# Sinkhorn-sorted attention and a bilinear feed-forward: pieces of unused matmuls, an early part of an output tile, and a token-on-partition mix for the last six pairs

## The chip, the cores and the metric

The kernel runs on one core of a Trainium2 chip. The metric is device time in microseconds (us) of one execution; lower is better. TensorE is called PE here (its weight loads PEld), VectorE DVE, ScalarE ACT, GpSimd POOL, and SyncE SP.

## The reference

Four batches, eight heads, 768 tokens, 64 elements a head. The tokens of a head stand in eight blocks of 96. Cut to what is computed:

```
P = sort_net                                  # 4 x 8 x 8 x 8
repeat 5 times:
    P = exp(P - rowmax);  P = P / rowsum;  P = P / columnsum
k_sorted = P mixes the 8 blocks of k;  v_sorted = P mixes the 8 blocks of v
scores = (q_block @ k_sorted_block^T) / 8     # inside each block of 96
attn   = softmax(scores)
x      = attn @ v_sorted_block                # 3072 tokens x 512
a = x @ w_a;  b = x @ w_b                     # 512 -> 1536
out = (a * b) @ w_out                         # 1536 -> 512, float32
```

## The kernel before, in words

Heads are worked on in pairs: pair g (0 to 15) has heads 2g and 2g + 1, and four pairs make a batch. Pair 0 to 3 is batch 0, and so on. All matmuls are bf16 with float32 sums.

The **Sinkhorn chain** (five rounds on ACT and DVE) comes first. Meanwhile PE does unused matmuls on a zero tile `warm` (`keep_busy`, L168) and turns q of the first pairs (`turn_q`). Each round after the first has one small matmul on `rsum`, so that the unused ones behind it start in step with the chain. The final P is spread by `to_columns` (L448) and `spread` into `s_all`, for each head a 128 x 128 matrix.

The **mix** multiplies it with k or v. A token's place in its 128-row chunk is on the partitions when it is loaded. `stage_mix` (L281) takes a 64-column chunk of k or v of one head as weights and `s_all` as the moving operand, 12 matmuls of 128 columns for k and 12 for v. The result has head elements on the partitions. ACT copies it into `kT`, DVE and ACT copy it into `vT`, in block order. v needs tokens on the partitions later: `turn_v` does this on PE for pair 4, a DMA transpose on the SP queue for pairs 5 and up, into `vs`. `stage_scores` (L302) then makes the scores and ACT the exponential `eT`; `stage_o` (L231, with `one_o`) multiplies with `vs` and DVE divides; `to_xT` sends the result through a DMA transpose into `xT`. Batch 0 is done in two halves of four blocks (`half_mix` to `half_x`), with PE transposes in place of the DMA's.

The **feed-forward** of batch b needs its `xT`. `ffn_ab` makes one step: eight matmuls of 384 columns (`ab_mms`, L332), four for a and four for b; ACT casts a (L352) and DVE multiplies into `hT` (L353). An output tile (`ffn_out`, L377) is two steps of six matmuls of 512 columns, then a copy to `o_sb` and a store. A batch has 24 such steps of the first kind and 12 of the second.

The **order** on PE, POOL, SP, ACT and DVE is written out by hand. While batch b's feed-forward runs, the attention of batch b + 1 is put between its steps: `units_full` lists units, c (mix), s (scores), o (output) of a pair, and `paced` spreads them over the steps. In the first batch some matmuls of the first feed-forward tiles are begun ahead (`begun`), three of their four parts each, and end later.

Loads with a cast from float32 go on POOL's queue. From pair 6 on, the mix of pair g is followed by a one-element POOL copy `gate` that waits for `kT`, and then by the load of pair g + 2, so that loads are not issued too early. q of pairs 6 and up is put in order by POOL (`pair_q`, L246) and turned by a DMA transpose (`stage_q`, L252). Buffers that matter: `kT`, `vT`, `eT`, `vs` have three each (pair number modulo 3), pool `psA` two PSUM tiles, `psF` four, `hT` two, `o_sb` three.

Of the kernel before, what the change touches and what calls it, by code (L numbers as in the profile page):

```python
# [9 lines left out]
FP32 = mybir.dt.float32  # L10
# [12 lines left out]
def kernel(  # L23
# [250 lines left out]
    def stage_mix(g, what, engines):  # L274
        src2 = loaded[g][0 if what == "k" else 1]
        to = (kTs if what == "k" else vTs)[g % NBUF]
        pitch, whole = (BLK, S + PAD) if what == "k" else (P, NB * P)
        mix = psA.tile([P, 2, 512], FP32, tag="A", name="mix")
        for c in range(NCH):
            for e in range(2):  # L280
                nc.tensor.matmul(  # L281
                    mix[e * D:(e + 1) * D, c // 3, c % 3 * P:(c % 3 + 1) * P],
                    lhsT=src2[:, e, c * D:(c + 1) * D],
                    rhs=s_all[:, 2 * g + e], start=True, stop=True)
        for hf, eng in enumerate(engines):
            n = 2 // len(engines)
            for u in range(n):
                d1 = _ap(to, (hf + u) * 3 * CG, [[whole, P], [CG, 3], [pitch, NB], [1, CG]])
                s1 = _ap(mix, (hf + u) * 512, [[1024, P], [P, 3], [CG, NB], [1, CG]])
                copy(eng, d1, s1)  # L290
        if what == "v" and g > HP:
            nc.sync.dma_start_transpose(out=vss[g % NBUF][:, :, V0:V0 + P],
                                        in_=to.rearrange("p i t -> p (i t)"))

    def stage_scores(g):
        kT, qT, eT = kTs[g % NBUF], st[g, "qT"], eTs[g % NBUF]
# [37 lines left out]

    def hT_of(b):
        if b not in hTs:
            hTs[b] = ffp.tile([P, KO, S], BF16, tag="hT", name="hT")
        return hTs[b]

    def ffn_ab(b, m, t, begun=()):  # L340
# [15 lines left out]
    def ffn_last(b, c):  # L356
        hT = hTs[b]
        rows = out[b * S:(b + 1) * S, :].rearrange("(p c) n -> c p n", c=NCH)
        for n0, n1, eng, queue in ((0, 384, "act", nc.sync), (384, DMODEL, "dve", nc.scalar)):
            po = psF.tile([P, 512], FP32, tag="F", name="po")  # L360
            for m in range(KO):
                nc.tensor.matmul(po[:, 0:n1 - n0], lhsT=hT[:, m, c * P:(c + 1) * P],  # L362
                                 rhs=w_out_sb[:, m, n0:n1], start=(m == 0), stop=(m == KO - 1))
            o_sb = ffp.tile([P, 512], FP32, tag="o_sb", name="o_sb", bufs=3)
            copy(eng, o_sb[:, 0:n1 - n0], po[:, 0:n1 - n0])
            queue.dma_start(out=rows[c][:, n0:n1], in_=o_sb[:, 0:n1 - n0])

# [14 lines left out]
        return [lambda: part(0), lambda: part(1)]  # L382

    def store(b, c, po):
        o_sb = ffp.tile([P, DMODEL], FP32, tag="o_sb", name="o_sb", bufs=3)
        copy("act" if c % 2 == 0 else "dve", o_sb, po)
        if b == 0:
            h, u = divmod(c, 3)
            for c2 in range(2):
                nc.sync.dma_start(  # L390
                    out=_ap(out, (h * PH * NCH + 2 * u + c2) * DMODEL,
                            [[NCH * DMODEL, PH], [1, DMODEL]]),
                    in_=o_sb[c2 * PH:(c2 + 1) * PH])
        else:
            rows = out[b * S:(b + 1) * S, :].rearrange("(p c) n -> c p n", c=NCH)
            nc.sync.dma_start(out=rows[c], in_=o_sb)


    with tc.manual_schedule(engines={ET.PE, ET.Pool, ET.SP}):
        with tc.manual_schedule(engines={ET.Activation, ET.DVE}):  # L400
# [3 lines left out]
            p_rep = const.tile([BH, NB * NB, CG // 2], FP32, name="p_rep")  # L404
            pc_ps = psA.tile([P, NB, BH], FP32, tag="A", name="pc_ps")
            heat = psA.tile([P, 2, 512], FP32, tag="A", name="heat")
            keep_busy(heat[:, 0], 8)
            for it in range(5):
                nc.scalar.activation(out=p_nat, in_=p_nat, func=AF.Exp)
                if it == 2:  # L410
                    turn_q(0, "act")
                if it == 3:
                    turn_q(1, "act")
                if it == 4:
                    turn_q(2, "act")
                    turn_q(3, "act")
                if it == 2:
                    with nc.allow_low_precision("sum of one one and zeros"):
                        nc.vector.reduce_sum(
                            out=mask, in_=_ap(ident, 0, [[P, P], [1, CG], [CG, NB]]),  # L420
                            axis=AX.X)
                nc.vector.reduce_sum(out=rsum, in_=p_nat, axis=AX.X)
                nc.vector.reciprocal(out=rsum, in_=rsum)
                if it > 0:
                    nc.tensor.matmul(heat[0:NB, 1, 0:NB], lhsT=rsum, rhs=rsum,
                                     start=True, stop=True)
                    keep_busy(heat[:, 0], (0, 4, 3, 2, 4)[it])
# [55 lines left out]
            half_o(0, 2)  # L483
            half_scores(0, 3)
            half_v(0, 3)
            half_x(0, 2, "act")
            half_o(0, 3)
            begun = [psF.tile([P, 512], FP32, tag="F", name="pf") for _ in range(3)]
            begun += [psA.tile([P, 2, 512], FP32, tag="A", name="two")[:, 0] for _ in range(2)]
            for n, (m, w_sb) in enumerate(((0, w_a_sb), (0, w_b_sb), (1, w_a_sb),  # L490
                                           (1, w_b_sb), (2, w_a_sb))):
                if n == 3:
                    half_x(0, 3, "act")
                ab_mms(begun[n], w_sb, 0, m, 0, range(KA - 1))


        for c in range(4, 6):
# [30 lines left out]
            us.append(lambda: half_x(1, HP - 1, "dve"))  # L528
            return us

        def units_full(b):
            g0, us = b * HP, []

            def c_(g):
                if g < 2 * HP - 2:
                    turn_q(g)
                stage_mix(g, "k", ("act",))
                stage_mix(g, "v", ("dve", "act"))
                if 2 * HP - 2 <= g < B * HP - 2:
                    nc.gpsimd.tensor_copy(out=gate, in_=kTs[g % NBUF][0:1, 0:1])  # L540
                    load_pair((g + 2) // HP, (g + 2) % HP)

            def s_(g):
                stage_scores(g)
                if g == HP:
                    turn_v(g)
                if g in (HP, HP + 1):
                    stage_q(g + 2)
                if 2 * HP <= g + 1 < B * HP:
                    pair_q(g + 1)  # L550
                    stage_q(g + 1)

            def o_(g):
                stage_o(g)
                to_xT(g)

            for u, n in ((c_, 0), (s_, 0), (c_, 1), (s_, 1), (c_, 2), (o_, 0), (s_, 2), (c_, 3),
                         (o_, 1), (s_, 3), (o_, 2), (o_, 3)):
                us.append(lambda u=u, g=g0 + n: u(g))
            return us  # L560

        def interleave(steps, units, spare, slow=0):
            n, done = len(steps), 0
# [4 lines left out]
                    units[done]()  # L568
                    done += 1

        def paced(ab, po, units, spare):
            steps = ab + po
            total = len(steps) - 2 * spare
            done = 0
            for now, step in enumerate(steps, 1):
                step()
                while done < len(units) and done * total < now * len(units):
                    units[done]()
                    done += 1

        steps = [lambda: ffn_ab(0, 0, 0, begun[0:2]), lambda: ffn_ab(0, 1, 0, begun[2:4]),
                 lambda: ffn_ab(0, 2, 0, begun[4:5])]
# [3 lines left out]
        for b in range(B):  # L586
            ab = [lambda m=m, t=t, b=b: ffn_ab(b, m, t)
                  for m in range(KO) for t in range(2) if b > 0 or t == 1]
            po = [f for c in range(NCH) for f in ffn_out(b, c)]
            paced(ab, po, units_full(b + 1) if b + 1 < B else [], 3 if b == 0 else 2)  # L590


# [28 lines left out]
```

The softmax here doesn't subtract the row's maximum and nothing guards it: scores larger than these inputs give would overflow.

## Time and profile before

| | |
|---|---|
| median of 12 runs | 245.81 us (245.53 to 246.31) |
| the profiled execution | 246.07 us |
| its span, first to last instruction | 244.3 us |
| PE busy | 237.0 us, 2234 matmuls |
| ACT, DVE, POOL busy | 104.5, 109.2, 61.5 us |
| granted TensorE clock | 1.0 |
| DMA transposes | 33 on SP's queue |
| last feed-forward of a batch ends near | 85, 139.6, 194 us for batches 0, 1, 2 |

Times inside the kernel count from the start of the span. In a view of the chain, a row has the start, the length, and the engine, tile and line; in a table of stretches the columns after the length are the busy times of PE, PEld, DVE, ACT and POOL, with the number of instructions in brackets, then the granted clock, the DMA engines' mean share and GB/s. A matmul's own duration is a latency: matmuls overlap in the array, so what one costs in a row of its like is the distance of the starts.

### The profile page before, as it was taken

Reading aid. Unit: us, or ns where it says so; the run is one execution under the profiler, and the core shown is the slowest. Engines: PE = TensorE matmul, PEld = TensorE weight load, DVE = VectorE, ACT = ScalarE, POOL = GpSimd, SP = SyncE. Lnnn points to the kernel's source line nnn. Section 1 sums busy time; section 2 is a strip of 40 time slices with the busy share of each in tenths; the row PEclk is TensorE's granted clock in tenths of the full one; section 3 lists DMA queues with packets and bytes.
Section 4 is the critical chain, followed back from the end, with each engine's and each line's share of the span. In section 5 each row is a group of like instructions: output and inputs, shape, how many; then the busy total and the mean of one; then the engine's idle time right before and its main releaser. Section 6 shows DMA issues by size and latency. Waiting matters only on the chain.

```text
span 244.3 us, 5487 instructions
## 1 busy us (share of the span) xinstructions
PE 237.0 (97%) x2234; PEld 137.0 (56%) x2246; DVE 109.2 (45%) x258; ACT 104.5 (43%) x204; POOL 61.5 (25%) x88
## 2 busy tenths in 40 slices
PE   7899999999999999999999999999999999999994
PEld 2466666666545466666654466666654465655442
DVE  6675466554436144454524234454525144344110
ACT  3664764466730065646430175636330133333001
POOL 8875579613230043240400053110000000000000
PEclk9999999999999999999999999999999999999999
DMA  5999999998999659994883457926224310000132
GB/s 80 201 198 197 197 200 201 202 119 84 168 152 195 137 97 126 157 150 70 120 131 118 119 101 123 157 54 67 43 79 122 114 46 0 0 3 1 43 129 86
DMA packets 53929, 28.02 MB, mean 115 GB/s; under 512 B 30736, under 2 KB 50960, under 8 KB 53904
## 3 DMA queue, kind: packets, MB, share of 16 engines
q0 software_dynamic: 20944, 14.16, 41.1%
q1 hardware_dynamic: 32816, 13.45, 28.9%
q8 instruction: 17, 0.28, 0.5%
q14 instruction: 8, 0.07, 0.1%
q10 hardware_dynamic: 144, 0.07, 0.1%
HBM read 28.32 MB, written 6.29 MB: 142 GB/s over the span
## 4 chain that ended last, share of the span: by engine, by line
PE 94%; DVE 3%; issue 1%; ACT 1%
PE pf L332 51%; PE po L377 24%; PE mix L281 4%; PE o_ps L231 3%; PE sc L302 2%; PE heat L168 2%; PE mixh L180 2%; PE po L362 1%; PE vs_ps L208 1%; PE sc L195 1%; PE xt_ps L222 1%; PE two L332 1%; PE q_ps L260 1%; DVE xp L237 1%; DVE o_sb L164 0%
## 5 line engine op out<-in xcount | busy, mean ns | idle before, releaser
L353 DVE TENSOR_TENSOR hT<-a_sb,pf 128x384 bf16<-128x384 bf16 x95 | 52.6, 554 | 73.8 <-PE pf L332 46.4
L332 PE MATMUL pf<-xT,w_a_sb 128*128 128x384 bf16 x380 | 77.9, 326 | 0.0
L332 PE MATMUL pf<-xT,w_b_sb 128*128 128x384 bf16 x380 | 77.4, 326 | 0.0
L352 ACT CAST a_sb<-pf 128x384 bf16<-128x384 f32 x95 | 45.5, 479 | 60.9 <-PE pf L332 41.3
L377 PE MATMUL po<-w_out_sb,hT 128*128 128x512 bf16 x265 | 61.3, 379 | 0.6
L332 PEld LDWEIGHTS <-w_b_sb 128*128 128x128 bf16 x384 | 37.5, 98 | 24.6
L332 PEld LDWEIGHTS <-w_a_sb 128*128 128x128 bf16 x384 | 34.9, 98 | 22.3
L377 PEld LDWEIGHTS <-hT 128*128 128x128 bf16 x276 | 26.2, 98 | 30.1
L162 ACT COPY o_sb<-po 128x512 f32<-128x512 f32 (+1 forms) x13 | 7.5, 578 | 46.8 <-PE po L377 45.2
L164 DVE COPY o_sb<-po 128x512 f32<-128x512 f32 (+1 forms) x12 | 7.9, 656 | 35.1 <-PE po L377 26.2
L307 ACT ACTIVATE eT<-sc 96x768 bf16<-96x768 f32 x24 | 18.1, 802 | 6.8 <-PE sc L302 6.8
L540 POOL COPY gate<-kT 1x1 bf16<-1x1 bf16 x8 | 1.4, 181 | 76.1 <-ACT kT L162 76.1
L237 DVE TENSOR_TENSOR xp<-o_ps,rec 96x512 bf16<-96x512 f32 x24 | 15.9, 684 | 0.6 <-DVE rec L235 0.2
L162 ACT CAST kT<-mix 128x384 bf16<-128x384 f32 x24 | 10.3, 482 | 7.9 <-PE mix L281 7.9
L95 POOL DMA_DIRECT2D k<-in_k_dram x16 | 11.6, 722 | 5.5 <-PE pf L332 2.3
L231 PEld LDWEIGHTS <-eT 96*128 96x128 bf16 x256 | 10.3, 97 | 3.1 <-DVE xp L237 0.6
L95 POOL DMA_DIRECT2D v<-in_v_dram x16 | 11.5, 718 | 2.1 <-PE pf L332 0.8
L235 DVE RECIPROCAL rec<-o_ps 96x8 f32<-96x8 f32 x32 | 5.6, 189 | 13.8 <-PE o_ps L231 13.8
L231 PE MATMUL o_ps<-vs,eT 96*128 96x65 bf16 x256 | 11.3, 193 | 0.1
L246 POOL COPY qc<-q 128x768 bf16<-128x768 bf16 x10 | 8.3, 834 | 8.1 <-DMA q<-in_q_dram 8.1
L168 PE MATMUL heat<-warm 128*128 128x512 bf16 x20 | 7.7, 530 | 1.4 <-DVE warm L77 1.3
L95 POOL DMA_DIRECT2D q<-in_q_dram x12 | 8.6, 713 | 1.5 <-DMA w_a_sb<-in_moe_w_a_dram 0.6
(80 smaller groups left out, 154.0 us busy)
## 6 DMA issues: line engine op xcount, KB each, us to landing
out_dram<-o_sb SPq DMA_DIRECT2D x17, 256.0 KB, 2.0
k<-in_k_dram POOLq DMA_DIRECT2D x16, 192.0 KB, 5.4
v<-in_v_dram POOLq DMA_DIRECT2D x16, 192.0 KB, 6.7
q<-in_q_dram POOLq DMA_DIRECT2D x12, 192.0 KB, 6.9
w_a_sb<-in_moe_w_a_dram POOLq DMA_DIRECT2D x6, 256.0 KB, 10.3
w_b_sb<-in_moe_w_b_dram POOLq DMA_DIRECT2D x6, 256.0 KB, 10.4
w_out_sb<-in_moe_w_out_dram POOLq DMA_DIRECT2D x3, 512.0 KB, 12.0
out_dram<-o_sb SPq DMA_DIRECT2D x12, 128.0 KB, 2.5
```

The source lines that it names most:

```text
L95: nc.gpsimd.dma_start(out=to, in_=_ap(t, base, [[W, P], [S * D, 2], [1, W]]))
L162: nc.scalar.copy(out=out, in_=in_)
L168: nc.tensor.matmul(ps[:, 0:cols], lhsT=warm[:, 0:P], rhs=warm[:, 0:cols], start=True, stop=True)
L231: nc.tensor.matmul(o_ps[:, e, i * (D + 1):(i + 1) * (D + 1)], lhsT=eT[:, hf, e, i * BLK:i * BLK + P], rhs=vs[0:BLK, i0 + i, V0 - 1 + e * ( ...
L237: nc.vector.tensor_tensor(out=_ap(xp, i0 * 2 * D, [[nxp * 2 * D, BLK], [D, 2], [2 * D, NBH], [1, D]]), in0=_ap(o_ps, 1, [[1024, BLK], [511 ...
L246: nc.gpsimd.tensor_copy(out=qc.rearrange("p c e d -> p e c d"), in_=loaded[g][2].rearrange("p e (c d) -> p e c d", c=NCH))
L281: nc.tensor.matmul(mix[e * D:(e + 1) * D, c // 3, c % 3 * P:(c % 3 + 1) * P], lhsT=src2[:, e, c * D:(c + 1) * D], rhs=s_all[:, 2 * g + e], ...
L307: nc.scalar.activation(out=eT[:, hf, :, 0:HB], in_=sc[0:BLK, :, 0:HB], func=AF.Exp, scale=float(scale))
L332: nc.tensor.matmul(pf[:, 0:HW], lhsT=w_sb[:, kc, m * P:(m + 1) * P], rhs=x_cols(b, kc, t), start=(kc == 0), stop=(kc == KA - 1))
L352: nc.scalar.copy(out=a_sb, in_=pf[:, 0:HW])
L353: nc.vector.tensor_mul(out=hT[:, m, t * HW:(t + 1) * HW], in0=a_sb, in1=ab[1][:, 0:HW])
L377: nc.tensor.matmul(held["po"], lhsT=hTs[b][:, m, c * P:(c + 1) * P], rhs=w_out_sb[:, m, :], start=(m == 0), stop=(m == KO - 1))
```

## The change

It has these parts.

1. The unused matmuls of the Sinkhorn chain, 8 + 4 + 3 + 2 + 4 of 512 columns, become 32 + 16 + 12 + 8 + 16 of 128. Those in `half_mix` stay.
2. Of the first begun feed-forward tile, the matmuls of its first two parts are issued between `half_v(0, 3)` and `half_x(0, 2)` of the first batch; the third follows where it was.
3. Pairs 10 to 15 (`plain`) are mixed by `stage_plain`: `s_all` is the weights and the whole 384 columns of a head the moving operand, two matmuls for k and two for v. Tokens then stand on the partitions. One copy (k, on ACT) or two (v, DVE and ACT) make `nat`; a DMA transpose turns it into `turned`; later POOL copies it in block order into `kT` or `vT` (`in_order`); for v the DMA transpose into `vs` follows as `return_v`.
4. For these pairs q is put in order and turned in the c unit itself.
5. The units are in one list with a batch for each. Batch 1's steps get 14 units, among them the mixes of pairs 12 and 13, the last one ahead of the last step; batch 2's get ten. For plain pairs, `in_order` comes after the unit that follows; the load of pair g + 2 comes after it, with no gate on `kT`; for pair 12 it is gated by the last part of the next batch's `xT`.
6. `hT` has one buffer instead of two, `o_sb` six instead of three.

```diff
+    def plain(g):
+        return g >= 2 * HP + 2
+
+    def stage_plain(g, what, engines):
+        src2 = loaded[g][0 if what == "k" else 1]
+        mix = psA.tile([P, 2, 512], FP32, tag="A", name="mix")
+        for e in range(2):
+            nc.tensor.matmul(mix[:, e, 0:W], lhsT=s_all[:, 2 * g + e], rhs=src2[:, e],
+                             start=True, stop=True)
+        nat = att.tile([P, NCH, 2, D], BF16, tag="nat", name="nat")
+        step = 2 // len(engines)
+        for u, eng in enumerate(engines):
+            copy(eng, nat[:, :, u * step:(u + 1) * step].rearrange("p c e d -> p e c d"),
+                 mix[:, u * step:(u + 1) * step, 0:W].rearrange("p e (c d) -> p e c d", c=NCH))
+        turned = att.tile([P, NCH, P], BF16, tag="turned", name="turned")
+        nc.sync.dma_start_transpose(out=turned, in_=nat.rearrange("p c e d -> p (c e d)"))
+        st[g, what] = turned
+
+    def in_order(g, what):
+        if what == "k":
+            to = kTs[g % NBUF][:, 0:S].rearrange("p (i c t) -> p c i t", i=NB, c=NCH)
+        else:
+            to = vTs[g % NBUF][:, :, 0:BLK].rearrange("p i (c t) -> p c i t", c=NCH)
+        nc.gpsimd.tensor_copy(out=to, in_=st[g, what].rearrange("p c (i t) -> p c i t", i=NB))
...
-            hTs[b] = ffp.tile([P, KO, S], BF16, tag="hT", name="hT")
+            hTs[b] = ffp.tile([P, KO, S], BF16, tag="hT", name="hT", bufs=1)
...
-            keep_busy(heat[:, 0], 8)
+            keep_busy(heat[:, 0], 32, P)
...
-                    keep_busy(heat[:, 0], (0, 4, 3, 2, 4)[it])
+                    keep_busy(heat[:, 0], (0, 16, 12, 8, 16)[it], P)
...
             half_v(0, 3)
+            begun = [psF.tile([P, 512], FP32, tag="F", name="pf")]
+            ab_mms(begun[0], w_a_sb, 0, 0, 0, range(2))
             half_x(0, 2, "act")
             half_o(0, 3)
-            begun = [psF.tile([P, 512], FP32, tag="F", name="pf") for _ in range(3)]
+            begun += [psF.tile([P, 512], FP32, tag="F", name="pf") for _ in range(2)]
...
-                ab_mms(begun[n], w_sb, 0, m, 0, range(KA - 1))
+                ab_mms(begun[n], w_sb, 0, m, 0, range(0 if n else 2, KA - 1))
...
+        def c_(g):
+            if g < 2 * HP - 2:
+                turn_q(g)
+            stage(g, "k", ("act",))
+            stage(g, "v", ("dve", "act"))
+            if plain(g):
+                pair_q(g)
+                stage_q(g)
+            else:
+                if g > HP:
+                    return_v(g)
+                if g >= 2 * HP - 2:
                     nc.gpsimd.tensor_copy(out=gate, in_=kTs[g % NBUF][0:1, 0:1])
+                    load_later(g)
...
+        plan(0, "c4", "s4", "c5", "s5", "c6", "o4", "s6", "c7", "o5", "s7", "o6", "o7")
+        plan(1, "c8", "s8", "c9", "s9", "c10", "o8", "c11", "o9", "s10", "c12", "s11", "o10", "o11",
+             "c13")
+        plan(2, "s12", "c14", "s13", "o12", "c15", "s14", "o13", "s15", "o14", "o15")
+        after = [[] for _ in seq]
+        for n, (b, u, g) in enumerate(seq):
+            if u is c_ and plain(g):
+                late = 3 if g % HP == 0 else 2
+                after[n + 1] += [lambda g=g, what=what: in_order(g, what) for what in "kv"]
+                if late == 3:
+                    after[n + 3].append(lambda g=g: nc.gpsimd.tensor_copy(
+                        out=gate, in_=xT_of(g // HP - 1)[0:1, HP - 1, 0:1]))
+                after[n + 2 * late - 3].append(lambda g=g: load_later(g))
+                after[n + late].append(lambda g=g: return_v(g))
...
-        def paced(ab, po, units, spare):
+        def paced(ab, po, units, spare, last):
             steps = ab + po
             total = len(steps) - 2 * spare
-            done = 0
+            main, done = len(units) - last, 0
             for now, step in enumerate(steps, 1):
                 step()
-                while done < len(units) and done * total < now * len(units):
+                while done < main and done * total < now * main:
                     units[done]()
                     done += 1
+                if now == len(steps) - 1 and last:
+                    units[main]()
...
-            paced(ab, po, units_full(b + 1) if b + 1 < B else [], 3 if b == 0 else 2)
+            paced(ab, po, units[b], 3 if b == 0 else 2, 1 if b == 1 else 0)
```

More of the change, by code (lines that the diff above doesn't have):

```diff
@@ L290, in stage_mix, with stage, return_v @@
                 copy(eng, d1, s1)
-        if what == "v" and g > HP:
-            nc.sync.dma_start_transpose(out=vss[g % NBUF][:, :, V0:V0 + P],
-                                        in_=to.rearrange("p i t -> p (i t)"))
+    def plain(g):
[14 more added lines that the diff above has]
+        st[g, what] = turned
+    def stage(g, what, engines):
+        (stage_plain if plain(g) else stage_mix)(g, what, engines)
+    def in_order(g, what):
[4 more added lines that the diff above has]
+        nc.gpsimd.tensor_copy(out=to, in_=st[g, what].rearrange("p c (i t) -> p c i t", i=NB))
+    def return_v(g):
+        nc.sync.dma_start_transpose(out=vss[g % NBUF][:, :, V0:V0 + P],
+                                    in_=vTs[g % NBUF].rearrange("p i t -> p (i t)"))
     def stage_scores(g):
@@ L363, in ffn_last @@
                                  rhs=w_out_sb[:, m, n0:n1], start=(m == 0), stop=(m == KO - 1))
-            o_sb = ffp.tile([P, 512], FP32, tag="o_sb", name="o_sb", bufs=3)
+            o_sb = ffp.tile([P, 512], FP32, tag="o_sb", name="o_sb", bufs=6)
             copy(eng, o_sb[:, 0:n1 - n0], po[:, 0:n1 - n0])
@@ L384, in store @@
     def store(b, c, po):
-        o_sb = ffp.tile([P, DMODEL], FP32, tag="o_sb", name="o_sb", bufs=3)
+        o_sb = ffp.tile([P, DMODEL], FP32, tag="o_sb", name="o_sb", bufs=6)
         copy("act" if c % 2 == 0 else "dve", o_sb, po)
@@ L529, in units_half @@
             return us
[L531 to L539, printed above, removed]
-                    nc.gpsimd.tensor_copy(out=gate, in_=kTs[g % NBUF][0:1, 0:1])
[L541 to L560, printed above, removed]
+        def c_(g):
[10 more added lines that the diff above has]
+                if g >= 2 * HP - 2:
+                    nc.gpsimd.tensor_copy(out=gate, in_=kTs[g % NBUF][0:1, 0:1])
+                    load_later(g)
@@ new lines, in s_, with o_, load_later, plan @@
+        def s_(g):
+            stage_scores(g)
+            if g == HP:
+                turn_v(g)
+            if g in (HP, HP + 1):
+                stage_q(g + 2)
+            if 2 * HP <= g + 1 < B * HP and not plain(g + 1):
+                pair_q(g + 1)
+                stage_q(g + 1)
+        def o_(g):
+            stage_o(g)
+            to_xT(g)
+        def load_later(g):
+            if g < B * HP - 2:
+                load_pair((g + 2) // HP, (g + 2) % HP)
+        seq = []
+        def plan(b, *names):
+            for name in names:
+                seq.append((b, {"c": c_, "s": s_, "o": o_}[name[0]], int(name[1:])))
@@ L562, in interleave, with unit @@
+        def unit(u, g, then):
+            u(g)
+            for f in then:
+                f()
+        units = [[] for _ in range(B)]
+        for (b, u, g), then in zip(seq, after):
+            units[b].append(lambda u=u, g=g, then=then: unit(u, g, then))
         def interleave(steps, units, spare, slow=0):
```

## The prediction

> **What bounds the kernel now.** I read the page first, then the chain of waits in order of time, then the timeline and the group rows of the stretches that the change touches, and last the DMA answers. The page's busy row and its chain say that TensorE (PE) is the limit nearly everywhere:
>
> ```profile
> PE 237.0 (97%) x2234; PEld 137.0 (56%) x2246; DVE 109.2 (45%) x258; ACT 104.5 (43%) x204; POOL 61.5 (25%) x88
> PE 94%; DVE 3%; issue 1%; ACT 1%
> ```
>
> A busy PE share alone proves little, so I look at starts. In the feed-forward steps eight matmuls of 384 columns take 1.30 us in the chain, 0.163 us each, back to back. Such steps and the output tiles fill the span from 12 us to the end. So a change pays only by taking columns off PE's stream or by closing the few holes in it. The chain has two holes in the first batch:
>
> ```profile
> 17.69 0.23 PE sc L195 x6
> 17.92 0.58 issue
> 18.50 0.22 PE sc L195 x2
> ...
> 20.39 0.70 DVE xph L237
> 21.09 0.05 issue
> 21.13 0.34 PE xt_ps L222 x4
> ```
>
> At 17.92 PE stops inside a run of eight score matmuls and waits for nothing that the profile shows. At 21.13 PE has waited for DVE's xph; the waits put 0.43 us of PE idle on it. The attention mix of a later pair (k and v, 24 matmuls) stands in the chain so:
>
> ```profile
> 139.65 1.30 PE pf L332 x8
> 140.95 0.79 PE mix L281 x24
> 141.74 2.71 PE pf L332 x16
> ```
>
> Two steps would be 2.60; the 0.11 over it is lost at the change of kind. A pair's mix thus costs 0.90 us of PE.
>
> **What the Trainium skill says.** (1) "TensorE: Matmul & The Clock Gate", Part 3: outputs narrower than 128 on different column groups run side by side. The trace agrees: 24 matmuls of 128 columns on 64-column weights take 0.79 us, 33 ns each, where the four 128-wide transposes at L208 start 60 ns apart. So the old mix is not as dear as its count. (2) Same page, Part 1: the cold array takes N ÷ 1.2 GHz. The eight 512-column unused matmuls start 0.427 us apart, which agrees. (3) Same page, Back-to-back issue gap: about 81 ns for a 128-column matmul with its own weights; the trace's 60 ns at L208 decides, 81 is my upper end. (4) "Runtime: NRT & Kernel Launch", Terms: instruction memory is refilled in 16 KiB blocks. The page's q8 row has 17 packets of together 0.28 MB, 16 KB each, for 4480 PE instructions: one per some 256.
>
> **Unused matmuls, 21 of 512 columns to 84 of 128.** The columns are the same. While cold, 32 pieces take what 8 took (3.42 us). Warm, a piece costs 60 ns against 54, so the last group of 16 lasts 0.96 instead of 0.86 us. It starts near 10.8 and is done near 11.75; the first column matmul (L448) waits for DVE's p_rep until 12.02. At 81 ns it would be done at 12.1, 0.1 late. Direct cost: 0, bounds 0 to +0.1; a clock released a window earlier or later would move it by -0.5 to +0.8, which the trace cannot exclude.
>
> The indirect effect is what I count. Each piece is two instructions, so PE's stream has 2 x 63 = 126 more ahead of the first mix. I read the 0.58 us as a late refill. By starts, 447 PE records precede the stop. The packet that starts in the DMA window 16.2 to 17.4 is a q8 packet. A block earlier, PE is 256 records back, at 12.85 us; from there to 18.50 is 5.65 us, my estimate of a refill's time under the weight loads (DMA share 1.38 between 12.85 and 17.92). PE ran through that block in 5.07 us. Moved by 126 instructions, the boundaries fall on what is now record 322, at 15.2 us, and 578, near 23. The block before 15.2 begins among the unused matmuls of the fourth round, near 9.2 us, because that part of the stream is slow: 6.0 us for its refill, 0.35 to spare. The next has 7.8, less 0.9 that is saved. The hole closes: **-0.58 us**, bounds 0 (not a refill, or it reappears) and -0.6.
>
> **Two matmuls of the first output tile between v and x.** They need the first two chunks of xT (DVE's copy ends at 20.24) and the first w_a slice, and run 0.33 us inside the 0.43 us hole. Behind them, seven instead of nine matmuls lie before the last half_x, which waits for xph (done 22.83): PE gets there at about 23.0 on the old clock, so no new wait. **-0.33 us**, bounds -0.1 (PSUM slot late) and -0.43.
>
> **Token-on-partition mix, pairs 10 to 15.** It removes 24 matmuls per pair (0.90 us) and puts four of 384 columns on full weights: 4 x 0.163 = 0.65, plus up to 0.11 at the change of kind. Saved 0.14 to 0.25 a pair, 0.2 taken: **-1.2 us** for six, bounds -0.8 and -1.5. ACT's k copy becomes one of 768 elements (nearest row eT: 802 ns) for two of 482; v's copies stay halved. These are hidden, ACT being 43% busy.
>
> New on SP: two DMA transposes a pair, 1.2 us of issue each; landing 2.9 to 7.4 us in the stretches from 85 to 168. New on POOL: two 128x768 copies a pair, 0.83 us each by the qc row. Scores of pair 10 come four units, about 15 us, after its mix; copy, issue, landing and POOL need about 1.5 + 1.2 + 6 + 2 = 11. Same for 11. POOL has no due work behind the copies except the loads of later pairs. SP's v return and stores queue behind the new transposes by at most 2.4 us; o_sb's six buffers cover the stores. hT with one buffer costs nothing: its first writer follows PE's new matmuls, which follow the last readers.
>
> **Moved units.** Batch 1 gets 13 units over the same 32 steps and one before the last step; pairs 12 and 13 come into it, batch 2 keeps ten. PE's sum is the same. Three waits get tighter. (a) s9 comes one step (1.3 us) earlier: its transpose is issued at 92.18 and took 5.4 us, so 97.6 against a PE arrival of 99.18: margin 1.6 becomes 0.3. (b) Pair 12's load waits on POOL for pair 10's copies; about 2 us of margin remain. (c) Pair 14's load is gated by the last xT. That was issued at 133.46, landed near 136.5, with batch 1 ending at 139.65; pair 13's mix now adds 0.7, so the gate opens 3.9 us before the end. v is issued 2.5 before the end and lands in 6.0 (the median of that stretch): 3.5 after it. PE reaches it four steps and one unit in, about 6.1 after: margin 2.6. I take **+0.2 us** for waits, bounds 0 and +6.
>
> **Sum.** -0.58 - 0.33 - 1.2 + 0.2 = -1.9 us. The profiled execution took 246.07 us (span 244.3 and 1.8 around it), 0.26 above the median of 245.81. So 244.2 for a like execution and **243.9** for a median. Differences below 0.2%, 0.5 us, count as none: that is about what a measurement of this kernel can tell.
>
> **Rivals.**
>
> *The transposes crowd out the loads.* The last q1 rows give about 0.66 us of all 16 engines per 256 KB store and, what is left, 1.5 us per transpose (36.9% of 55 us, less six stores, over 11). From pair 10's mix to the end of batch 1 the trace has these rows:
>
> ```profile
> 101.00:121.00 20.00, 20.00 (x201) 12.54 (x199) 10.53 (x23) 10.29 (x22) 6.32 (x10) 1.00 0.84 116
> 121.00:139.60 18.60, 18.44 (x128) 9.21 (x130) 6.25 (x13) 3.93 (x7) 0.00 (x0) 1.00 0.61 132
> ```
>
> The last two columns are DMA share and GB/s. To 28 us of share come eight new transposes, two for q and one for v that move in, 16.5 us: 44.5 in 39.5. As bytes that is 4.77 + 2.17 MB, 176 GB/s. For it: that is over a share of 1, and loads took up to 9.7 us in crowded stretches. Against it: the start of the kernel moved 199 GB/s at a share of 1.38, and the new transfers have slack. It decides at place (c): a v landing of 8.6 us is free, 10.7 eats the whole gain of 2.1, and at 12.5 the stall is 3.9: 243.7 + 3.9 = **247.6**, slower.
>
> *The refill hole only moves.* Then 0.33 + 1.2 - 0.2 = -1.3: **244.5**. For it: 0.35 us is little to spare, and my boundary rests on counting records, of which a few are missing. Against: both blocks get longer times than the 5.07 us of the one that ran dry.
>
> *The mix saves nothing.* If each full-weight load is laid bare (98 ns, PEld rows), four cost 1.04 a pair against 0.90: +0.8 for six, and with the other terms +0.1 in all: **245.9**, no change. Against: the steps' own loads are 98 ns too, and hide at 0.163 a matmul.
>
> *The reorder does not do what it says.* If the early tile finds no free PSUM slot, PE waits for DVE's vs copy (ends 21.41) and xt slips by 0.3: 243.9 + 0.6 = **244.5**.
>
> **How the numbers follow.** My forecast, 243.9, gets 0.48 (own range 243.2 to 244.7). Hole moves or reorder fails: 0.22, still faster. Mix saves nothing: 0.08, half of it within 0.5 us and half, with the loads only partly bare, still faster. Crowding: 0.22, of which 0.03 stays faster and 0.02 within. So faster 0.77, same 0.06, slower 0.17. The range runs from 242.7 (all gains at their upper bounds: 0.6 + 0.43 + 1.5, clock a window early 0.5) to 246.5, where crowding above it, 0.16, and about 0.04 below are left out.
>
> **What would show it.** Right: no "issue" piece near 17.9 and none of 0.5 us elsewhere in the first 30 us; two pf matmuls ahead of the third xt_ps run; 24 mix matmuls of 384 columns, at 0.65 to 0.75 us a pair in the chain; 12 new transposes landing in under 8 us. Wrong: PE waiting for k or v from DRAM ahead of pair 14's mix, for qTf at s9, or for kT from POOL; a mix pair still at 0.9; q_ps or p_rep's matmuls later than 6.8 and 12.0. A time above 246.3 would refute the forecast.

## The result and the profile after

The changed kernel takes **243.52 us** (243.28 to 243.97) where the kernel before took 245.82 in the same comparison: a ratio of 0.9903, with a 95% interval of 0.9894 to 0.9912. The forecast was 243.9 in a range of 242.7 to 246.5. The profiled execution took 243.66 us with a span of 241.9, against 246.07 and 244.3 before: 2.4 us less in the trace.

The page's busy row and the shares of its chain, after:

```profile
PE 235.8 (97%) x2179; PEld 140.6 (58%) x2189; DVE 109.1 (45%) x258; ACT 104.1 (43%) x198; POOL 70.3 (29%) x97
PE 94%; DVE 3%; ACT 1%; issue 1%; DVEq 0%
```

TensorE (PE) still sets the end. POOL is busy 8.8 us longer: twelve copies of 0.83 us are new, and three of the one-element `gate` copies are gone. The first batch in the chain of waits of the kernel after (start, us, what):

```profile
17.67 0.28 PE sc L195 x8
...
19.71 0.70 DVE xph L237
...
20.46 0.36 PE xt_ps L222 x4
...
20.84 0.49 ACT xT L162
...
21.37 1.30 PE pf L361 x7
22.67 0.17 PE xt_ps L222 x4
```

The eight score matmuls now run without the stop, in 0.28 us; cut in two by it they took 0.23 and 0.22 beside the stop itself. The two early feed-forward matmuls are done while DVE works on xph, so they are on no line here. But the chain now goes over ACT's copy of the third part of xT, which it did not touch before. PE's timeline of the kernel after (start, us, instruction, wait ahead of it) has the wait:

```profile
20.78 0.41 PE L231 MATMUL o_ps<-vs,eT 96*128 96x65 bf16 x8
21.37 0.32 PE L361 MATMUL pf<-xT,w_a_sb 128*128 128x384 bf16 x1 [0.18 <-ACT xT L162]
```

In the kernel before, the first feed-forward matmul started 0.24 us after the o_ps run (21.46 to 21.70); here it is 0.59. The difference of 0.35 is the 0.33 of the two matmuls that stood there. A new mix, same view:

```profile
99.54 0.81 PE L361 MATMUL pf<-xT,w_b_sb 128*128 128x384 bf16 x4
100.19 0.49 PE L299 MATMUL mix<-k,s_all 128*128 128x384 bf16 x2
100.52 0.49 PE L299 MATMUL mix<-v,s_all 128*128 128x384 bf16 x2
100.84 0.81 PE L361 MATMUL pf<-xT,w_a_sb 128*128 128x384 bf16 x4
```

The four mix matmuls of 384 columns take 0.65 us from their first start to the next feed-forward matmul's (100.19 to 100.84), 0.163 us each, as the four feed-forward matmuls ahead of them do (99.54 to 100.19). So nothing is lost at the change of kind.

Where the 2.4 us come from, by starts in the two chains:

| place | before | after | gained up to here |
|---|---|---|---|
| first column matmul (pc_ps) | 12.02 | 11.99 | 0.03 |
| third xt_ps | 21.13 | 20.46 | 0.67 |
| fourth xt_ps | 23.34 | 22.67 | 0.67 |
| start of batch 1 | 85.13 | 84.46 | 0.67 |
| start of batch 2 | 139.65 | 139.78 | -0.13 |
| start of batch 3 | 194.17 | 192.02 | 2.15 |
| end of PE's last matmul | 240.95 | 238.80 | 2.15 |
| end of the span | 244.3 | 241.9 | 2.4 |

Batch 1 is 0.80 us longer and batch 2 2.28 shorter, since pairs 12 and 13 moved. Together that is 1.48 for six pairs, 0.25 a pair. The rest, about 0.25, lies after the last matmul and was not followed up.

### The profile page after: what moved, and what is told of

The parts are those of the page before. It is cut to its first block, busy times and chain, and to the rows that moved or that the text cites. A ratio compares the mean times of both kernels' runs of the same rounds, so it can differ in the third digit from the quotient of the medians.

```text
span 241.9 us, 5392 instructions
## 1 busy us (share of the span) xinstructions
PE 235.8 (97%) x2179; PEld 140.6 (58%) x2189; DVE 109.1 (45%) x258; ACT 104.1 (43%) x198; POOL 70.3 (29%) x97
## 4 chain that ended last, share of the span: by engine, by line
PE 94%; DVE 3%; ACT 1%; issue 1%; DVEq 0%
PE pf L361 52%; PE po L406 24%; PE o_ps L231 3%; PE sc L331 2%; PE heat L168 2%; PE mix L281 2%; PE mixh L180 2%; PE mix L299 2%; PE po L391 1%; PE vs_ps L208 1%; PE xt_ps L222 1%; PE sc L195 1%; PE two L361 1%; PE q_ps L260 1%; DVE xp L237 1%
## 5 line engine op out<-in xcount | busy, mean ns | idle before, releaser
L318 POOL COPY kT<-turned 128x768 bf16<-128x768 bf16 x6 | 5.0, 830 | 31.5 <-PE pf L361 8.0
L95 POOL DMA_DIRECT2D v<-in_v_dram x16 | 11.5, 718 | 3.1 <-DMA w_b_sb<-in_moe_w_b_dram 1.3
L574 POOL COPY gate<-kT 1x1 bf16<-1x1 bf16 x4 | 0.7, 180 | 33.3 <-ACT kT L162 33.3
L162 ACT CAST nat<-mix 128x768 bf16<-128x768 f32 (+1 forms) x12 | 7.7, 639 | 4.2 <-PE mix L299 3.5
L168 PE MATMUL heat<-warm 128*128 128x128 bf16 x84 | 8.0, 273 | 1.3 <-DVE warm L77 1.3
```

Source lines behind the costliest of these rows:

```text
L95: nc.gpsimd.dma_start(out=to, in_=_ap(t, base, [[W, P], [S * D, 2], [1, W]]))
L162: nc.scalar.copy(out=out, in_=in_)
```

## The experiments

Two theories were to be told apart. **A**, the forecast's: the stop at 17.9 us is a late refill of PE's instructions, and the pieces end it because they put more instructions ahead of it; the mix saves PE time pair by pair; the reorder fills a hole. **B**: the width of the pieces or the reorder ends the stop, or the mix gains more than it seems and the transposes take part of it back. Medians and ratios are to the kernel before, on the same chip.

### The parts of the start alone

`p1_128` is the kernel before with the pieces only, 126 PE instructions more:

```
-keep_busy(heat[:, 0], 8)
+keep_busy(heat[:, 0], 32, P)
-    keep_busy(heat[:, 0], (0, 4, 3, 2, 4)[it])
+    keep_busy(heat[:, 0], (0, 16, 12, 8, 16)[it], P)
```

> The kernel before with part 1 alone (all unused matmuls in pieces of 128 columns; 126 PE instructions more ahead of the first mix). Refill theory: the 0.58 us stop at 17.9 us is a late refill of PE's instruction memory, and goes; 0.6 to 0.75 us faster, first column matmul still near 12.0, no stop of over 0.3 us before 30 us. Rival (the width matters, by an earlier full clock or a shorter Sinkhorn chain): the gain shows ahead of 12.6 us, where the first mix starts earlier.

Measured: 245.09 us, 0.9969 [0.9961, 0.9978]. The stop is gone (chain of waits):

```profile
11.69 0.28 PE pc_ps L448 x4
...
17.37 0.28 PE sc L195 x8
```

`p1_256` does the same in pieces of 256 columns, 42 instructions more:

```
+keep_busy(heat[:, 0], 16, 256)
+    keep_busy(heat[:, 0], (0, 8, 6, 4, 8)[it], 256)
```

> The kernel before with the unused matmuls in pieces of 256 columns (42 PE instructions more ahead of the first mix, a third of the change's). Refill theory by counting: the block before the critical boundary now begins at what was record 150, at 11.0 us, its refill is in by 16.65, and PE gets to the boundary (record 406) at 16.9: no stop, so the same gain as with 128 columns, 0.6 to 0.75 us. Rival (width of the pieces): about a third to a half of the gain of 128 columns.

Measured: 245.11 us, 0.9972 [0.9960, 0.9985]; no stop either.

`p1_24` cuts only the group of the second round, four of 512 columns into sixteen of 128: 24 instructions more.

```
+    keep_busy(heat[:, 0], (0, 16, 3, 2, 4)[it], P if it == 1 else 512)
```

> The kernel before with only the second group of unused matmuls (4 of 512) in 16 pieces of 128 columns (24 PE instructions more). Refill theory by counting: the block begins at what was record 168, at 12.25 us, its refill is in by 17.9, PE gets to the boundary (record 424) at 17.3: a stop of about 0.5 us stays, near 17.3 us, inside the work some 24 instructions earlier (xt_ps or o_ps in place of sc); time within 0.25 us of before. Rival (width of the pieces): part of the gain, no stop.

Measured: 245.07 us, 0.9968 [0.9956, 0.9981]. Where the forecast's counting put a stop of 0.5 us at 17.3, there is none (chain of waits):

```profile
12.29 0.27 PE pc_ps L448 x4
...
17.96 0.28 PE sc L195 x8
```

From its first column matmul to the end of its last matmul PE takes 228.28 us in `p1_24`, `p1_256` and `p1_128`, to the hundredth, and 228.93 in the kernel before. So neither the width nor the number matters once the stop is gone.

`p2_only` is the kernel before with the reorder only:

```
+begun = [psF.tile([P, 512], FP32, tag="F", name="pf")]
+ab_mms(begun[0], w_a_sb, 0, 0, 0, range(2))
 half_x(0, 2, "act")
...
-        ab_mms(begun[n], w_sb, 0, m, 0, range(KA - 1))
+        ab_mms(begun[n], w_sb, 0, m, 0, range(0 if n else 2, KA - 1))
```

> The kernel before with part 2 alone (the first two parts of the first begun tile between the v and x work). The prediction's step: 0.33 us faster. What the trace after suggests: nothing (within 0.1 us), since the next matmul of that tile needs the third part of xT, which ACT copies until 0.3 us after the o_ps matmuls; PE fills one hole and gets another of about 0.3 us ahead of the pf matmuls.

Measured: 245.81 us, 0.9998 [0.9989, 1.0008]: nothing gained. Its chain of waits:

```profile
17.30 0.23 PE sc L195 x6
17.54 0.96 issue
18.50 0.22 PE sc L195 x2
...
21.13 0.36 PE xt_ps L222 x4
...
21.52 0.49 ACT xT L162
...
22.05 1.30 PE pf L332 x7
23.34 0.17 PE xt_ps L222 x4
```

The fourth xt_ps starts at 23.34, exactly as before the reorder: what the early matmuls save behind the third xt_ps is lost to the wait for ACT. PE also resumes at 18.50 as in the kernel before, although this execution came to the stop 0.38 us earlier (17.54 against 17.92): the stop did not end earlier for an earlier arrival.

`after_512` is the changed kernel with the unused matmuls at 512 columns again:

```
-keep_busy(heat[:, 0], 32, P)
+keep_busy(heat[:, 0], 8)
-    keep_busy(heat[:, 0], (0, 16, 12, 8, 16)[it], P)
+    keep_busy(heat[:, 0], (0, 4, 3, 2, 4)[it])
```

> The changed kernel with part 1 undone (unused matmuls of 512 columns again). Refill theory: the stop comes back between 17 and 18.5 us, 0.6 to 0.9 us long, and the kernel takes 0.65 to 0.8 us more than the changed one (about 244.2). Rival (the stop had to do with the order of the work, which the change also altered): no stop, 243.5.

Measured: 244.41 us, 0.9933 [0.9918, 0.9948]. The stop is back (chain of waits):

```profile
17.91 0.23 PE sc L195 x6
18.14 0.88 issue
19.02 0.22 PE sc L195 x2
```

The pieces' 0.31% and this kernel's 0.67% add to 0.98%, the change's 0.97%. With the reorder at nothing, the 0.67% belongs to the mix together with what was changed for it (parts 3 to 6); no run has the mix without the rest.

**What follows for the stop.** It goes with 24, 42 or 126 more instructions in three widths, and returns when they are taken out. The DMA rows show what goes with it: the first 16 KB packet of row q8, taken for PE's instructions because the row's 16 to 18 packets match PE's count at about 256 each, starts at 16.27 us in the kernel before, 16.04 in `p2_only` and 16.65 in `after_512`, and PE resumes 2.23, 2.46 and 2.37 later. Without a stop it starts at 14.20 (`p1_24`), 13.06 (`p1_256`), 11.21 (`p1_128`) and 11.38 (the changed kernel): the more instructions ahead, the earlier. "Runtime: NRT & Kernel Launch" (Terms) of the Trainium skill has instruction memory refilled in 16 KiB blocks, which the 16 KB packets agree with. That PE waits for this very packet no record states; everything here fits it, but the cause is inferred.

### The order of the begun tiles

`after_kc` tries to win what the reorder missed. The first two chunks of tiles 1 and 2 also go ahead of the third part of xT:

```
+for n in (1, 2):
+    ab_mms(begun[n], firsts[n][1], 0, firsts[n][0], 0, range(2))
+for n in range(3):
+    ab_mms(begun[n], firsts[n][1], 0, firsts[n][0], 0, range(2, KA - 1))
+half_x(0, 3, "act")
+for n in (3, 4):
+    ab_mms(begun[n], firsts[n][1], 0, firsts[n][0], 0, range(KA - 1))
```

> The changed kernel with the begun tiles' matmuls in another order: behind the o_ps matmuls first the four that need only the first two parts of xT (tiles 1 and 2), then the third parts of tiles 0 to 2. Theory: the change's part 2 gains nothing because the next matmul waits for ACT's copy of the third part of xT; with this order PE fills both holes: 0.33 us faster than the changed kernel, the last half_x near 22.2 in place of 22.5. Rival (xph of the last pair is done too late): PE gets to the last half_x early and waits for xph, gain 0.1 or less.

Measured: 243.59 us, 0.9903 [0.9890, 0.9916], the changed kernel's own ratio. The wait for ACT is filled (chain of waits). Counted from the first column matmul, the fourth xt_ps comes 0.34 us earlier than in the changed kernel (after 10.34 us, not 10.68):

```profile
20.40 0.34 PE xt_ps L222 x4
20.75 0.39 PE o_ps L231 x8
...
22.27 0.23 PE xt_ps L222 x4
```

Later it goes again. The waits of the changed kernel have PE's weight load held for pair 9's turned q for 0.3 us, and PE itself for nothing; in `after_kc` the same row (in total, times, longest) has more, and PE itself waits 0.19 us:

```profile
PEld L331 <- DMA qTf<-qc: 0.6, 1, 0.6
```

The transpose is issued 0.34 us earlier than in the changed kernel (91.15 against 91.49), but lands 5.86 us after its issue, and pair 10's mix stands at 100.28 against 100.36. What was won is waited away at a margin of 0.3 us.

`after_kc_q9` therefore turns pair 9's q right after pair 7's output (issued at 78.03, 13 us earlier):

```
-if 2 * HP <= g + 1 < B * HP and not plain(g + 1):
+if g + 1 == 2 * HP:
...
+if g == 2 * HP - 1:
+    pair_q(g + 2)
+    stage_q(g + 2)
```

> The reordered begun tiles, and q of pair 9 put in order and turned right after pair 7's output instead of after pair 8's scores. Theory: the 0.33 us that the reorder won in the first batch was given back at pair 9's scores, where PE waits for the transpose of q; with that issued some 14 us earlier it stays: 0.3 us faster than the changed kernel (243.2). Rival: the gain is lost elsewhere (another wait between 85 and 140 us), and it stays at 243.5.

Measured: 243.54 us, 0.9893 [0.9875, 0.9911]. In the trace PE needs 226.52 us from its first column matmul to its last, against 226.81 in the changed kernel, and PE waits no more for q there. Such 0.3 us the timing can't tell from none.

### More pairs in the new form

`after_plain8` mixes pairs 8 and 9 in the new form too, which at 0.25 us a pair should give 0.5 us:

```
-return g >= 2 * HP + 2
+return g >= 2 * HP
...
+plan(0, ..., "o7", "c8")
+plan(1, "c9", "s8", "c10", "s9", "o8", "c11", "s10", "o9", "c12", "s11", "o10", "o11", "c13")
...
-    late = 3 if g % HP == 0 else 2
+    late = 3 if g == 3 * HP else 2
...
-paced(ab, po, units[b], 3 if b == 0 else 2, 1 if b == 1 else 0)
+paced(ab, po, units[b], 3 if b == 0 else 2, 1 if b < 2 else 0)
```

> The changed kernel with pairs 8 and 9 mixed in the new way too, pair 8's mix ahead of the last step of batch 0, units re-planned (c8 in batch 0; c9 s8 c10 s9 o8 c11 s10 o9 c12 s11 o10 o11 and last c13 in batch 1). If a pair's mix costs PE 0.65 in place of 0.90 us and the transposes stay covered: 0.5 us faster than the changed kernel (243.0). Rival (four more DMA transposes crowd batch 1, whose DMA share is already 0.89 between 100.4 and 139.8): PE waits for a load or a kT, and the gain is lost.

Measured: 248.36 us, 1.0082 [1.0052, 1.0112]: slower than the kernel before by 0.8%. Its chain of waits:

```profile
85.35 2.78 DMA turned<-nat
...
88.28 0.83 POOL vT L318
89.10 0.66 POOL k L95
...
90.14 7.45 DMA v<-in_v_dram
...
97.64 0.50 PE mix L299 x2
```

Pair 10's v is issued by POOL, in order behind pair 8's copies, which wait for the transposes. It lands 7.45 us after its issue, when PE has waited 3.20. That is not all of the loss. The timeline of PE after it:

```profile
97.64 0.50 PE L299 MATMUL mix<-v,s_all 128*128 128x384 bf16 x2 [3.20 <-DMA v<-in_v_dram]
97.98 1.41 PE L361 MATMUL pf<-xT,w_a_sb 128*128 128x384 bf16 x4
...
101.61 0.81 PE L361 MATMUL pf<-xT,w_b_sb 128*128 128x384 bf16 x4
```

Twelve matmuls take 3.63 us (97.98 to 101.61) where twelve otherwise take 1.96 (12 x 0.163): the granted clock is 0.50 between 99 and 101 us. By starts PE loses 3.37 us at this mix, 1.67 in the twelve matmuls and 0.30 at pair 8's scores, which wait for q. That is 5.3; less the 0.5 that two more new mixes save it is the 4.85 by which PE's way from first column to last matmul is longer. Two of the six executions kept a mean granted clock of 1.000, where the other four have 0.993; they took 246.41 and 246.99 us, so what the lower clock costs shows in the times too.

`after_kc_plain8` puts both edits together.

> Both of the last two edits together. If each holds, their sum: 0.8 us faster than the changed kernel (242.7). If one fails, the other's share alone.

Measured: 248.60 us, 1.0110 [1.0095, 1.0124]. PE waits there for the same load, and the clock falls again: 0.34 us won at the start doesn't touch it.

`after_kc_p8early` takes away what delays the load. Pair 10 is loaded after pair 7's output and pair 11 in unit c9, both before POOL's copies that wait:

```
+if g == 2 * HP + 1:
+    load_later(g)
...
+if g == 2 * HP - 1:
+    load_later(2 * HP)
...
-after[n + 2 * late - 3].append(lambda g=g: load_later(g))
+if g > 2 * HP + 1:
+    after[n + 2 * late - 3].append(lambda g=g: load_later(g))
```

> Pairs 8 and 9 mixed in the new way as well, with the reorder, and with the loads of pairs 10 and 11 issued before POOL's waits (after pair 7's output and in pair 9's mix). Theory: the 6.5 us that the first try of pair 8 lost were one late load (pair 10's v, queued on POOL behind the copies of pair 8); with the loads early the mix gains come through: 0.7 to 0.8 us faster than the changed kernel (242.8). Rival (DMA engines crowded by the transposes themselves): PE still waits for kT, qT or v in batch 1 and the kernel takes 244 or more.

Measured: 243.29 us, 0.9899 [0.9874, 0.9924]. This edit is the only difference to `after_kc_plain8`, and the 5 us are back, so the place of the load in POOL's order was the cause. In the trace PE takes 226.39 us from first column to last matmul, 0.42 less than in the changed kernel, where 0.5 + 0.34 was to be had. The waits of batch 1 show where some of it goes: s8 now waits for POOL's vT and for q.

```profile
PEld L331 <- POOL vT L318: 0.7, 1, 0.7
PE sc L331 <- DMA qTf<-qc: 0.3, 1, 0.3
```

`best_q8` wanted those too and turned q of pairs 8 and 9 right after pair 7's output.

```
+if g > 2 * HP + 1:
     pair_q(g)
     stage_q(g)
...
+for n in (2 * HP, 2 * HP + 1):
+    pair_q(n)
+    stage_q(n)
```

> As the last one (pairs 8 and 9 mixed in the new way, reorder, early loads of pairs 10 and 11), with q of pairs 8 and 9 put in order and turned right after pair 7's output. Theory: what was left of PE's waits in batch 1 (about 0.6 us at the scores of pair 8, for the transpose of q and for POOL) goes: PE's time from the first column matmul to its last comes to about 225.9 us (226.8 in the changed kernel), 242.7 in all. Rival: the two q transposes, ahead of eight stores on SP, delay pair 8's own k and v transposes, and the waits move to kT: 243.3 or more.

Measured: 246.27 us, 1.0000 [0.9978, 1.0023]: in the median all of the gain is gone. The profiled execution is the fastest of them, 244.77 us. Its chain of waits:

```profile
75.92 9.84 DMA xT<-xp
...
85.80 0.97 PE pf L361 x5
```

The transpose of pair 7's x, which batch 1 begins with, lands 9.84 us after its issue, and PE waits 0.90 us for it; another 0.91 go at pair 8's scores, to POOL's copy into kT. The two transposes of x between 74 and 86 us take 6.9 and 9.8 us here and 2.8 and 2.9 in the changed kernel, which has neither the early loads nor the q transposes beside them. In `after_kc_p8early`, with early loads alone, they take 9.4 and 6.9, and PE doesn't wait; which neighbour does it is not separated. What the median loses beyond this execution, 1.5 us, no trace shows. No version beyond the change is clearly faster than it.

### Twice the transposes

`after_double` does every new k and v transpose a second time, into a tile that nothing reads; o_sb has five buffers in place of six to make room. It was meant to test the crowding rival.

```
+again = att.tile([P, NCH, P], BF16, tag="again", name="again", bufs=1)
+nc.sync.dma_start_transpose(out=again, in_=nat.rearrange("p c e d -> p (c e d)"))
```

> The changed kernel with every new k and v transpose done twice (the second into a tile that nobody reads; o_sb has five buffers in place of six for the space). It adds 12 DMA transposes and 2.4 us of SP issue a pair, as much again as the change itself added. If the margins that the changed trace shows (1.9 us for pair 14's v, over 5 us for the scores) cover it: within 0.5 us of the changed kernel. If the crowding rival is only just avoided: PE waits 2 us or more at pair 14's mix or at a score unit, and the time is back at 245.5 to 248.

Measured: 255.01 us, 1.0364 [1.0327, 1.0400]. The stretch from pair 10's mix to the end of batch 1 (busy times, then clock, DMA share, GB/s), in the changed kernel and in this one:

```profile
100.40:139.80 39.40, 39.24 (x295) 22.09 (x297) 17.72 (x37) 16.18 (x29) 13.85 (x19) 1.00 0.89 148
```

```profile
100.40:139.80 39.40, 38.63 (x293) 21.61 (x292) 17.23 (x37) 15.38 (x29) 10.82 (x14) 1.00 0.98 153
```

In this stretch the two hardly differ: PE waits 0.77 us in it, at 131.83, for v's return. Most of the waits come later (PE's timeline):

```profile
97.33 0.51 PE L333 MATMUL sc<-qTf,kT 64*128 64x96 bf16 x16 [0.39 <-DMA qTf<-qc]
...
142.90 0.32 PE L363 MATMUL pf<-xT,w_a_sb 128*128 128x384 bf16 x1 [1.50 <-DMA xT<-xp]
150.69 0.50 PE L299 MATMUL mix<-v,s_all 128*128 128x384 bf16 x2 [2.04 <-DMA v<-in_v_dram]
159.20 0.52 PE L333 MATMUL sc<-qTf,kT 64*128 64x96 bf16 x16 [2.43 <-DMA qTf<-qc]
```

With the 0.77 these are 7.1 us; the first of them lies ahead of the first added transpose (103.00). After the 2.04 the clock drops again: the next twelve matmuls take 3.63 us (151.02 to 154.65), 1.7 too long. PE's way from first column to last matmul is 9.4 us longer; the other 0.6 is spread, and 1.6 us lie after the last matmul and were not followed up.

But these waits do not show that the DMA engines are too full. SP issues its transposes in order, and the added ones all write one buffer, `again`, so each waits until the one before has landed. SP's waits of this run, and its timeline (start, us of issue):

```profile
SPq L309 <- DMA again<-nat: 10.8, 6, 5.3
```

```profile
139.27 1.28 SPq L349 DMA_TRANSPOSE xT<-xp  x1
...
145.94 1.42 SPq L307 DMA_TRANSPOSE turned<-nat  x1
152.77 1.21 SPq L309 DMA_TRANSPOSE again<-nat  x1
154.07 1.24 SPq L252 DMA_TRANSPOSE qTf<-qc  x1
```

The same in the changed kernel:

```profile
132.94 1.78 SPq L347 DMA_TRANSPOSE xT<-xp  x1
...
142.26 2.86 SPq L252 DMA_TRANSPOSE qTf<-qc  x1
```

The x transpose behind the 1.50 is issued 6.3 us later than in the changed kernel and takes 3.58 us (3.37 there). The v behind the 2.04, whose gate waits for that x, is issued 6.5 us later and takes 6.79 (6.51). The q behind the 2.43 is issued 11.8 us later and takes 4.99 (4.91). So three of the waits, 6.0 of the 7.1 us, come from late issue, with at most 0.3 us more in the transfer itself. The new transposes do land more slowly, in 6.1 us in the median against 4.1, but what that alone would cost this run does not separate. And a high share is not enough for a wait: in the changed kernel it is 1.02 from 142 to 150 us and 1.45 from 150 to 155, and PE waits for nothing there.

## Why the prediction was right, point by point

**The refill stop: -0.58 predicted, -0.65 to -0.75 found** (0.67 in the two traces, of which 0.03 were there at the first column matmul; 0.31% of 245.8 in `p1_128`). The term counted the stop alone, without the score matmuls that it cut in two. The mechanism is inferred, not recorded, and no run speaks against it, but the counting of block boundaries was off: by the same counting `p1_24` should have had a stop of 0.5 us at 17.3. The packet starts above fit best, by an estimate that counts the records of the seven traces, a trigger some 20 records earlier than the forecast's, with 3.0 to 3.8 us from there to the packet; where it sits exactly stays open. The rival of a hole that only moves fell: no execution with more instructions ahead shows a stop in the first batch.

**The reorder: -0.33 predicted, 0 found.** This is the step that failed, at "PE gets there at about 23.0 on the old clock, so no new wait". It looked at the last half_x only. The first of the seven matmuls in front of it needs the third part of xT. In the kernel before, ACT's copy of it ended at 21.99 (21.51 + 0.48), and after the two moved matmuls the first that needs it came at 22.03 (21.70 + 2 x 0.163): they stood exactly in that gap, and without them PE waits for the same copy. The timeline of the kernel before, ACT and PE:

```profile
21.51 0.48 ACT L162 COPY xT<-xt_ps 128x384 bf16<-128x384 bf16 x1 [0.23 <-PE xt_ps L222]
```

```profile
21.70 0.67 PE L332 MATMUL pf<-xT,w_a_sb 128*128 128x384 bf16 x3
```

`p2_only` shows both sides of the exchange in one chain. The rival for this part named PE waiting for DVE's vs copy; that is not what happened.

**The mix: -1.2 predicted, -1.48 found.** Right in kind, and mis-sized by the 0.11 us at the change of kind: about half of it was taken to remain in the new form, and there it doesn't occur (0.65 us for four, 0.163 each). The upper bound of 1.5 is what came. The rival in which the weight loads lie bare is refuted by the same rows.

**The waits: +0.2 predicted, none to be found in the end.** Margin (a), q at s9, was forecast at 0.3; q was issued at 91.49, took 5.3, and PE came at 97.14: 0.3. Margin (c), pair 14's v, was forecast at 2.6: the gate opened 3.4 us before the batch's end rather than 3.9, v landed after 6.5 rather than 6.0, at 143.8, and PE came to it at 145.70: 1.9 left.

**The unused matmuls themselves: 0 predicted, 0 found.** The last sixteen start 60 ns apart, and the column matmul behind them starts at 11.99, when p_rep is there, as before. "TensorE: Matmul & The Clock Gate" (Back-to-back issue gap) has 81 ns for 128 columns; here the trace's 60 decides.

**The crowding rival** had a chance of 0.22 and was over-sized: 44.5 us of share in 39.5 was forecast, 0.89 x 39.4 = 35.1 measured, 148 GB/s and not 176. Two reasons: pair 13's transposes, issued at 139.03, fall almost wholly behind the stretch, as does its q, and 1.5 us a transpose, read from old rows, was probably too much. Whether crowding as such is near stays open: `after_double` is 11.5 us over the change for twelve transposes more, but mostly because SP issues late what stands behind them; `best_q8` has landings of x that grow from 2.9 to 9.8 us and cost PE 0.90. The rival also priced its stall without the clock that falls after it, which takes 1.7 us in `after_plain8`.

**The sum.** -0.67 + 0 - 1.48 + 0 = -2.15 against -1.9, and about 0.25 at the span's end that no step had: -2.4 in the trace, -2.3 in the medians. That the total came so near is in part luck: the 0.33 that the reorder didn't bring was made up by a larger mix, waits that didn't come and the 0.25 at the span's end.

## What to carry to other kernels

Before matmuls are moved into a hole, look up what they covered where they stood: here they covered ACT's copy, and the move exchanged one wait for another of the same size. A stop of PE that has no releaser in the profile can be a matter of how many instructions lie ahead of it; a few dozen more, placed where PE is slow, are a cheap test. Narrow margins on transfers (0.3 us at s9) decide what the next gain on PE is worth, and POOL's order decides when a load starts: check what a load is queued behind before work with waits is put on that queue. SP's queue is the same for transposes: a test that adds transfers also delays the issue of all that stands behind them, and so does not by itself tell a full DMA from a full queue.

## What the runs showed of the hardware

- The stop ends 2.2 to 2.5 us after the start of PE's 16 KB instruction packet (three executions), not a fixed time after PE's arrival: it ended at 18.50 in two executions that came to it 0.38 us apart. So it also swallows differences at the start: first column matmuls at 12.02 (before) and 11.63 (`p2_only`) both lead to a last matmul ending at 240.95.
- After a wait of PE of 3.20 us the next twelve matmuls ran at half clock, and likewise after one of 2.04, but not after one of 2.43 in the same execution. "TensorE: Matmul & The Clock Gate" (Why this matters for your kernels) warns of gaps over about 3 us; one of 2.04 was enough here. The traces' record of the granted clock shows a pattern. In all fourteen traces it changes only at whole multiples of 3.41 us from its first entry: in `after_double` at 4.46, 151.23 (43 x 3.41 later) and 154.65. A drop between matmuls lasts one such step, and half of 3.41 is the 1.7 us that it cost. Cut into these steps, the wait of 2.04 lies whole in the step that ends at 151.23, while the one of 2.43 is split into 1.29 and 1.14. Every step from 12 us on in which PE idled for 2.04 us or more (up to 3.41, the ends of the kernels included) was followed by half clock, and none with 1.90 or less was. So, in these traces, what counts is the idle time within a step. This is read from the traces; no run was made to test it.
- Transposes by DMA suffer from company: x transposes land in 2.8 and 2.9 us with few neighbours and in 6.9 to 9.8 beside early loads (`after_kc_p8early`) or early loads and other transposes (`best_q8`).
- A transpose takes SP 1.2 us or more to issue (1.21 the least in `after_double`), and SP issues in order: with twelve more on SP, and 10.8 us of waits for their one buffer, a q transpose was issued 11.8 us later and landed as fast as before (4.99 us, 4.91 without them).
